# A first token list from 96 columns, a third list for the rest, six rounds for seven, and raw weights issued by ScalarE

## The chip, the cores and the metric

The kernel runs on one core of a Trainium2 chip. The core has TensorE (PE; the profile shows its weight loads apart, as PEld), VectorE (DVE), ScalarE (ACT), GpSimd (POOL) and SyncE (SP), which here only issues DMAs. ACT and POOL issue DMAs too. The metric is the time of one launch in device microseconds (us). Lower is better.

## The reference

An attention of fixed weights, a causal convolution of seven taps per head, is followed by a mixture of experts in which the (token, expert) pairs are taken greedily in the order of their logits, each token once and each expert up to its capacity.

```python
def reference(**kwargs):
    attn_out = _attn_ref(**attn_kwargs)            # [8, 3584, 192], softmax of 7 taps per head
    return _moe_ref(x=attn_out.reshape(28672, 192), **moe_kwargs)

def _moe_ref(x, w_gate, w1, w2):                   # w_gate 192x8, w1 8x192x1024, w2 8x1024x192
    cap = N // E                                   # 28672 / 8 = 3584
    logits = x @ w_gate
    order = np.argsort(-logits.flatten())
    for idx in order:
        tok, e = (int(idx) // E, int(idx) % E)
        if assigned[tok] >= 0 or counts[e] >= cap:
            continue
        assigned[tok] = e
        counts[e] += 1
    for e in range(E):
        mask = assigned == e
        out[mask] = np.maximum(x[mask] @ w1[e], 0.0) @ w2[e]
```

## The kernel before

**First stage.** The attention is computed in 16 tiles of 1792 rows. For each, conv(i) multiplies the rows X with a banded matrix TH, head by head (PE, tile cv), ACT copies the result from four PSUM banks to a, and a is stored to the DRAM tensor attn by ACT's queue. The rows of tile i + 3 are loaded at the start of tile i, by SP's and ACT's queues. Two tiles later the gate follows: DVE transposes a (transp, four steps, tile aT), PE makes the logits from it (gate, three steps of two matmul groups each, tile pl), and end(i) brings them into the table LT and takes the maximum over the experts (M1). LT holds 256 columns of 128 tokens, 16 columns a tile. These small steps stand in a list, left, that mid(h) works off beside conv, one step a head, and from tile LAG = 13 on only once the first list of tokens is made (got), then two steps a head.

**Lists.** A second program, bg, runs beside both stages as a chain of generators (line 1537), worked off a step at a time by hook in the first stage and by steps in the second. A model of the engines' times, Pace, decides while the program is written how many steps go in. The chain before is half(0), tail, half(1), rest. half(0) finds the threshold Ts from a sample of the first 96 columns (thresh), waits for column 128, and makes the list of the tokens above Ts in columns 0 to 127: settle marks them (F), count counts them, place numbers them with matmuls, slots splits the numbers, sort writes each token into its place with one-hot matmuls (tiles oa and X, one matmul for each column), turn transposes, gather collects and tokens turns it into row numbers (ia, ja). When it is done, first() gathers the rows of the first two FFN tiles, and todo transposes the first of them within the loop or behind it. tail makes the logits of the last two tiles. half(1) lists columns 128 to 255 in the same way, but with sort4, which turns its table through DRAM (otab) and lets other steps run meanwhile; before, these are open(), which opens the table for the rounds. rest runs the rounds (seven by ROUNDS), which settle the thresholds of all experts, then final, and the last lists, twice sort4.

**FFN.** Second stage: 56 tiles of 512 tokens; the first eight are one for each expert from the first list, the next 24 need the second list, the last 24 the last lists. Each takes 40 matmuls to the hidden layer (l1, tile ph; ACT writes hh, DVE the remainder hl) and 64 back (l2, tile y). Numbers are kept as high and low parts. Rows are gathered two tiles ahead by POOL; tile 8's gather, at the start of tile 6, is where the second list must be there (drain in idx_of), tile 32's, at the start of tile 30, the last one. In tiles 0 to 7 the weights come in as raw pieces, eight an expert: wsplit, once a step of eight in a tile, splits a piece on ACT and DVE, stores both parts to DRAM for later (kw, kd, kv), and calls wload, which loads the piece that takes the freed buffer, of four. All of these DMAs are issued by SP, in the order of the program. An issue on SP stands behind the copies that wait for their split. From tile 8 on the kept parts are read back.

If the checks at the end of the lists find a count that does not fit (bad), a general path follows that does everything again.

```python
ROUNDS = [(8, 1.0, False, 16)] + [(16, 1.0, False, 8)] * 2 + [(16, 0.5, True, 8)] * 2 + [(0, 0.0, True, 8)] * 2
...
        bg = Steps(nc, r, (half(0), tail(), half(1), rest()))
...
        self.done += 1
        self.wload()
```

Of the kernel before, what the change touches and what calls it, by code (L numbers as in the profile page):

```python
# [245 lines left out]
TA = 16  # L246
TB = 12

ROUNDS = [(8, 1.0, False, 16)] + [(16, 1.0, False, 8)] * 2 + [(16, 0.5, True, 8)] * 2 + [(0, 0.0, True, 8)] * 2
# [10 lines left out]
class Route:  # L260
# [15 lines left out]
    def consts(self):  # L276
# [12 lines left out]
        self.g1 = cst.tile([128, 2], F32, name="g1")  # L289
        for h in range(2):  # L290
            P.tensor_scalar(self.g1[:, h:h + 1], pf, 1.0 + 128 * h, None, op0=OP.add)
# [81 lines left out]
    def settle(self, h):  # L373

        V, wk = self.nc.vector, self.wk
        s = slice(128 * h, 128 * h + 128)
        yield "cols", 128 * h + 128
        if h == 0:
            self.F = wk.tile([128, 8, G], BF, name="F")
        m = wk.tile([128, 128], F32, name="m_f")  # L380
        V.scalar_tensor_tensor(m, self.M1[:, s], self.Ts, self.M1[:, s], op0=OP.is_lt, op1=OP.add)
        for q in range(2):
            e = slice(4 * q, 4 * q + 4)
            V.tensor_tensor(self.F[:, e, s], self.LT[:, e, s], m[:, None, :].to_broadcast([128, 4, 128]),
                            op=OP.is_equal)
            yield PEW if q else None


    def count(self, F, h):
        nc, wk = self.nc, self.wk  # L390
        V, PE = nc.vector, nc.tensor
        s = slice(128 * h, 128 * h + 128)
        if h == 0:
            self.tot = [None, None]
            self.sl = wk.tile([128, G], F32, name="sl")
        ps = self.bg()
        for e in range(8):
            PE.matmul(ps[:, e:e + 1], F[:, e, s], self.ones[:, 0:1], start=True, stop=True, skip_group_check=True)
        t = self.tot[h] = wk.tile([128, 8], BF, name="tot%d" % h)
        nc.scalar.activation(t, ps[:, 0:8], AF.Copy)  # L400
        yield PEA

    def place(self, F, h, base):
# [3 lines left out]
        s = slice(128 * h, 128 * h + 128)  # L407
        SP = wk.tile([128, 8, 128], F32, name="X0")
        for q in range(2):
            ps = self.bg()  # L410
            f = F[:, 4 * q:4 * q + 4, s]
            PE.matmul(ps, self.U, f, start=True, stop=False, skip_group_check=True)
            for u in range(4):
                e = 4 * q + u
                o = ps[:, 128 * u:128 * u + 128]
                b = lambda t: t[:, e:e + 1].to_broadcast([128, 128])
                if base is not None:
                    PE.matmul(o, b(self.tot[base]), self.ones, start=False, stop=False, skip_group_check=True)
                PE.matmul(o, b(self.tot[h]), self.U, start=False, stop=(u == 3), skip_group_check=True)
# [1286 lines left out]
```

## Time and profile before

| | us |
|---|---|
| three runs | 1254.54, 1260.52, 1265.29 |
| median | 1260.52 |
| profiled execution, its own time | 1251.99 |
| its span | 1250.2 |
| first hidden-layer write (hh) of tile 0 | 164.24 |
| of tile 8 | 324.16 |
| of tile 26 | 664.75 |
| of tile 30 | 758.64 |

Nearly all instructions go through the helper in line 56 (Meter), so groups are told apart by the names of what they write and read: "ph<-xa,w" is the hidden layer's matmul. In the rows of a timeline stand the start, the length, the engine, the shapes, how many were merged and, in brackets, the idle time ahead and who ended it. In the rows of windows stand the busy time and the number of instructions of PE, PEld, DVE, ACT and POOL, then the granted clock, the share of the DMA engines and GB/s. In the rows of waits stand the total, the number and the longest.

### The profile page before, as it was taken

Reading aid. Unit: us, or ns where it says so; the run is one execution under the profiler, and the core shown is the slowest. Engines: PE = TensorE matmul, PEld = TensorE weight load, DVE = VectorE, ACT = ScalarE, POOL = GpSimd, SP = SyncE. Lnnn points to the kernel's source line nnn. Section 1 sums busy time; section 2 is a strip of 40 time slices with the busy share of each in tenths; the row PEclk is TensorE's granted clock in tenths of the full one; section 3 lists DMA queues with packets and bytes.
Section 4 is the critical chain, followed back from the end, with each engine's and each line's share of the span. In section 5 each row is a group of like instructions: output and inputs, shape, how many; then the busy total and the mean of one; then the engine's idle time right before and its main releaser. Section 6 shows DMA issues by size and latency. Waiting matters only on the chain.

```text
span 1250.2 us, 21752 instructions
## 1 busy us (share of the span) xinstructions
PE 1208.1 (97%) x7702; PEld 1036.5 (83%) x7702; DVE 979.4 (78%) x2131; ACT 547.4 (44%) x1220; POOL 531.7 (43%) x528
## 2 busy tenths in 40 slices
PE   4999989999999999999999989999999999999997
PEld 2445568889988989889888879999999999999996
DVE  7388669889898898989888865777777777777772
ACT  4454555656444544444543333333443333443331
POOL 3000344535455545555454434445444544444522
PEclk9999999999999999999999999999999999999999
DMA  9999889999725463444344563114133222413100
GB/s 221 339 348 310 294 299 316 280 321 302 270 82 155 128 188 113 158 149 149 123 144 135 178 164 121 36 48 154 67 126 107 95 97 96 157 56 137 49 23 28
DMA packets 125188, 205.09 MB, mean 164 GB/s; under 512 B 21440, under 2 KB 85392, under 8 KB 121360
## 3 DMA queue, kind: packets, MB, share of 16 engines
q1 hardware_dynamic: 82464, 127.22, 31.9%
q0 software_dynamic: 21504, 44.07, 11.7%
q10 hardware_dynamic: 21104, 32.34, 7.8%
q8 instruction: 62, 1.02, 0.3%
q14 instruction: 54, 0.44, 0.1%
HBM read 118.64 MB, written 84.93 MB: 163 GB/s over the span
## 4 chain that ended last, share of the span: by engine, by line
PE 85%; DVE 6%; DMA 5%; issue 1%; SPq 1%; ACT 1%; POOL 1%; ACTq 0%; POOLq 0%; DVEq 0%
PE ph L56 40%; PE y L56 38%; PE bg L56 3%; PE cv L56 3%; DMA X<-in_x_dram 2%; DVE X L56 1%; DVE aT L56 1%; DMA wgr<-in_moe_w_gate_dram 1%; DMA raw<-in_moe_w_dram 1%; DMA X<-otab 1%; PE pl L56 1%; DMA xg<-attn,ja 1%; DVE hl L56 0%; PE px L56 0%; DMA otab<-X 0%
## 5 line engine op out<-in xcount | busy, mean ns | idle before, releaser
L56 PE MATMUL y<-w,hh 128*128 128x384 f32 x1792 | 536.8, 355 | 0.0
L56 ACT ACTIVATE hh<-ph 128x512 fp32r<-128x512 f32 x448 | 267.2, 597 | 486.3 <-PE ph L56 485.2
L56 PE MATMUL y<-w,hl 128*128 128x192 f32 x1792 | 449.7, 251 | 0.0
L56 DVE SCALAR_TENSOR_TENSOR hl<-ph,hh 128x512 fp32r<-128x512 f32 x448 | 308.5, 689 | 138.6 <-ACT hh L56 134.0
L56 PE MATMUL ph<-xa,w 128*128 128x512 f32 x1344 | 395.6, 402 | 0.0
L56 PEld LDWEIGHTS y<-w,hl 128*128 128x128 f32 x1792 | 341.7, 191 | 16.4
L56 PEld LDWEIGHTS y<-w,hh 128*128 128x128 f32 x1792 | 337.1, 188 | 20.4 <-issue 2.2
L56 PEld LDWEIGHTS ph<-xa,w 128*128 128x128 f32 x1344 | 218.9, 189 | 20.2 <-issue 1.0
L1348 POOL DMA_INDIRECT out_dram<-yo,ia x128 | 138.9, 1085 | 225.9 <-DVE yo L56 188.1
L1348 POOL DMA_INDIRECT out_dram<-yo,ib x96 | 95.9, 999 | 220.1 <-DVE yo L56 212.7
L56 PE MATMUL ph<-xd,w 128*128 128x512 f32 x448 | 178.9, 399 | 1.3 <-DVE xd L56 1.3
L56 PE MATMUL ph<-xd,dl 128*128 128x512 f32 x448 | 174.6, 390 | 0.2 <-DVE dl L56 0.2
L56 DVE STREAM_TRANSPOSE xs<-xg 32x128 f32<-32x128 f32 (+2 forms) x408 | 164.8, 404 | 6.6
L1273 POOL DMA_INDIRECT xg<-attn,ja x128 | 139.3, 1088 | 47.6 <-issue 40.4
L56 PE MATMUL cv<-X,TH 118*128 118x384 f32 x256 | 101.5, 523 | 19.5 <-DVE TH L56 12.5
L1273 POOL DMA_INDIRECT xg<-attn,jb x96 | 103.4, 1078 | 29.3 <-issue 29.3
L56 ACT ACTIVATE yt<-y 128x192 f32<-128x192 f32 x224 | 73.1, 326 | 94.3 <-PE y L56 92.3
L56 DVE TENSOR_TENSOR yo<-y,yt 128x192 f32<-128x192 f32 x224 | 79.5, 355 | 41.3 <-ACT yt L56 39.2
L56 PEld LDWEIGHTS ph<-xd,w 128*128 128x128 f32 x448 | 84.3, 188 | 21.4 <-DVE xd L56 1.7
L56 PEld LDWEIGHTS ph<-xd,dl 128*128 128x128 f32 x448 | 84.5, 189 | 19.7 <-issue 0.5
L56 PEld LDWEIGHTS cv<-X,TH 118*128 118x128 f32 x256 | 45.3, 198 | 49.9 <-issue 14.1
L56 ACT ACTIVATE a<-cv 128x384 f32<-128x384 f32 x128 | 59.5, 492 | 50.8 <-PE cv L56 33.0
(238 smaller groups left out, 893.1 us busy)
## 6 DMA issues: line engine op xcount, KB each, us to landing
attn<-a ACTq DMA_DIRECT2D x16, 1344.0 KB
w<-kw SPq DMA_DIRECT2D x14, 1536.0 KB
w<-kv SPq DMA_DIRECT2D x14, 1536.0 KB
kw<-w SPq DMA_DIRECT2D x48, 256.0 KB
kv<-w SPq DMA_DIRECT2D x32, 384.0 KB
X<-in_x_dram SPq DMA_DIRECT2D x17, 672.0 KB
X<-in_x_dram ACTq DMA_DIRECT2D x15, 672.0 KB
scr<-xs SPq DMA_DIRECT2D x96, 96.0 KB
```

The lines of the kernel that those rows point to most:

```text
L56: return f(*a, **k)
L1273: self.nc.gpsimd.indirect_dma_start(out=t[:, b], out_offset=None, in_=self.attn[0:rows], in_offset=bass.IndirectOffsetOnAxis(ap=idx[b], ax ...
L1348: st = self.nc.gpsimd.indirect_dma_start(out=self.out, out_offset=bass.IndirectOffsetOnAxis(ap=idx, axis=0), in_=o, in_offset=None, bounds ...
```

## The change

- **First list.** The columns are cut in PARTS, (0, 96), (96, 128) and (224, 32), given as first column and number. early makes the first list from the first part, so it waits for column 96 only. second lists the second part with sort4, with third (settle, count and counts for the last part) in its waiting time, and then the last part with sort and turn. The generators take a part and the parts ahead of it in place of a half and its base; their matmuls are as wide as the part. open() moves to the head of rest. The last lists stay halves (HALVES).
- **Rounds.** One of the two rounds (16, 1.0, False, 8) goes.
- **Raw weights.** wload issues on ACT's queue. wsplit no longer calls it at its end, but notes that a load is owed, and the next call of wsplit issues it first. The copies kept in DRAM (the parts) stay on SP's.
- **Logits.** From tile 13 on the three gate steps of a tile are one step, put ahead of the transposes.

```diff
+PARTS = ((0, 96), (96, 128), (224, 32))
+HALVES = ((0, 128), (128, 128))
+
+ROUNDS = [(8, 1.0, False, 16)] + [(16, 1.0, False, 8)] + [(16, 0.5, True, 8)] * 2 + [(0, 0.0, True, 8)] * 2
...
-    def settle(self, h):
+    def settle(self, part):
         V, wk = self.nc.vector, self.wk
-        s = slice(128 * h, 128 * h + 128)
-        yield "cols", 128 * h + 128
+        c0, n = part
+        s = slice(c0, c0 + n)
+        yield "cols", c0 + n
...
+                for p in bases:
+                    m = p[1]
+                    PE.matmul(o, self.tot[p][:, e:e + 1].to_broadcast([m, 128]), self.ones[0:m, 0:n],
+                              start=False, stop=False, skip_group_check=True)
+                PE.matmul(o, self.tot[part][:, e:e + 1].to_broadcast([n, 128]), self.U[0:n, 0:n],
+                          start=False, stop=(u == 3), skip_group_check=True)
...
-    def lists(self, F, nt, h, base, idx, row, *part, between=None, swap=False):
-
-        nc = self.nc
-        yield from self.place(F, h, base)
-        yield from self.slots(F, h, between is None)
+    def listed(self, F, nt, part, bases, between=None):
+
+        yield from self.place(F, part, bases)
+        yield from self.slots(F, part, between is None)
         if between is None:
-            yield from self.sort(h, nt, base)
-            yield from self.turn()
+            yield from self.sort(part, nt, bases)
+            yield from self.turn(part[1])
         else:
-            yield from self.sort4(h, nt, base)
+            yield from self.sort4(part, nt, bases)
             yield from between
-        yield from self.gather(nt, base is None)
-        yield from self.tokens(nt, idx, row, *part, swap=swap)
+        yield from self.gather(part[1], nt, not bases)
...
         if what == "a":
-            nc.sync.dma_start(t, self.w1[e, 0:128, s])
+            nc.scalar.dma_start(t, self.w1[e, 0:128, s])
         elif what == "d":
-            nc.sync.dma_start(t[0:64], self.w1[e, 128:192, s])
-            nc.sync.dma_start(t[64:128], self.w1[e, 128:192, s])
+            nc.scalar.dma_start(t[0:64], self.w1[e, 128:192, s])
+            nc.scalar.dma_start(t[64:128], self.w1[e, 128:192, s])
         else:
-            nc.sync.dma_start(t[:, 0:2 * D].rearrange("p (k d) -> p k d", d=D),
+            nc.scalar.dma_start(t[:, 0:2 * D].rearrange("p (k d) -> p k d", d=D),
...
     def wsplit(self, i, eng):
 
+        if self.owed:
+            self.wload()
+        self.owed = False
         if self.done == len(self.pieces) or self.pieces[self.done][0] > i:
             return
...
         self.done += 1
-        self.wload()
+        self.owed = True
...
-        def half(h):
-            if h == 0:
-                yield from r.thresh(0.905)
-            yield from r.settle(h)
-            yield from r.count(r.F, h)
-            if h:
-                yield from r.counts(NE)
-            yield from r.lists(r.F, TA, h, 0 if h else None, *((ia, ja) if h else (ia0, ja0, 8, 4)),
-                               between=r.open() if h else None, swap=h == 1)
+        def early():
+            yield from r.thresh(0.905)
+            yield from r.settle(PARTS[0])
+            yield from r.count(r.F, PARTS[0])
+            yield from r.listed(r.F, TA, PARTS[0], ())
+            yield from r.tokens(TA, ia0, ja0, 8, 4)
+
+        def second():
+            yield from r.settle(PARTS[1])
+            yield from r.count(r.F, PARTS[1])
+            yield from r.listed(r.F, TA, PARTS[1], PARTS[0:1], between=third())
+            yield from r.listed(r.F, TA, PARTS[2], PARTS[0:2])
+            yield from r.tokens(TA, ia, ja, swap=True)
+
+        def third():
+            yield from r.settle(PARTS[2])
+            yield from r.count(r.F, PARTS[2])
+            yield from r.counts(NE)
 
         def rest():
+            yield from r.open()
             yield from r.rounds()
...
-        bg = Steps(nc, r, (half(0), tail(), half(1), rest()))
+        bg = Steps(nc, r, (early(), tail(), second(), rest()))
...
+        def gates(i):
+            for u in range(3):
+                gate(i, u)
...
                 if i and h == 0:
+                    if i >= LAG:
+                        left.append(partial(gates, i - 2))
                     for u in range(4):
                         left.append(partial(k.transp, i - 1, u))
-                        if i > 1:
+                        if 1 < i and (u == 3 or i < LAG):
                             left.append(partial(gate, i - 2, u) if u < 3 else partial(end, i - 2))
```

155 lines of the change are left out of this document (81 added, 74 removed).

## The prediction

> **What bounds the kernel now.** I read the page first: the engines' shares and the chain that ended last.
>
> ```profile
> span 1250.2 us, 21752 instructions
> PE 1208.1 (97%) x7702; PEld 1036.5 (83%) x7702; DVE 979.4 (78%) x2131; ACT 547.4 (44%) x1220; POOL 531.7 (43%) x528
> PE 85%; DVE 6%; DMA 5%; issue 1%; SPq 1%; ACT 1%; POOL 1%; ACTq 0%; POOLq 0%; DVEq 0%
> ```
>
> TensorE (PE) carries the chain. Then I cut the span by stage: the last part of the first stage, in which attention and the first list share PE (to 164.2); FFN tiles 0 to 7, which read and split the weights; tiles 8 to 25, beside which the rounds run; tiles 26 to 29, beside which the last lists are made; and the rest. The second fence counts the hidden layer's (hh) instructions in the same stretches: ACT writes eight a tile. The last two columns are the DMA engines' share and GB/s: they are full up to tile 7 and not after.
>
> ```profile
> 99.20:164.20 65.00, 60.09 (x585) 35.76 (x588) 47.81 (x88) 32.36 (x81) 17.85 (x18) 1.00 0.92 286
> 164.20:324.10 159.90, 156.68 (x1103) 137.41 (x1100) 140.52 (x291) 92.24 (x199) 69.60 (x62) 1.00 0.95 312
> 324.10:664.70 340.60, 339.74 (x1962) 304.40 (x1961) 300.23 (x689) 155.37 (x382) 180.81 (x163) 1.00 0.46 142
> 664.70:758.60 93.90, 90.11 (x739) 78.47 (x738) 71.64 (x145) 37.05 (x73) 38.96 (x36) 0.96 0.54 157
> 758.60:1216.00 457.40, 457.40 (x2603) 415.29 (x2602) 344.60 (x733) 175.54 (x351) 202.27 (x196) 1.00 0.27 92
> ```
>
> ```profile
> 164.20:324.10 159.90, 68.38 (x225) 42.26 (x225) 43.21 (x63) 37.95 (x64) 1.00 0.95 312
> ...
> 664.70:758.60 93.90, 39.65 (x129) 24.71 (x128) 21.99 (x32) 19.16 (x32) 0.96 0.54 157
> 758.60:1216.00 457.40, 237.68 (x801) 150.17 (x801) 138.37 (x200) 119.48 (x201) 1.00 0.27 92
> ```
>
> A tile that nothing disturbs takes 457.4/25 = 18.3 us, and the change does not touch it. The excess is what can move: 159.9 - 8 x 18.3 = 13.5 us in tiles 0 to 7, 340.6 - 18 x 18.3 = 11.2 in 8 to 25, 93.9 - 4 x 18.3 = 20.7 in 26 to 29, and whatever the first stage wastes. So I asked last what PE itself waited for, from 96 to 190 us (four rows), from 190 to 325 (one) and after (last row).
>
> ```profile
> PE bg L56 <- DVE F L56: 1.7, 2, 1.3
> PE pl L56 <- DVE aT L56: 1.6, 3, 0.8
> PE bg L56 <- DMA xg<-attn,ja: 1.5, 1, 1.5
> PE ph L56 <- DVE xd L56: 1.3, 1, 1.3
> PE bg L56 <- DMA raw<-in_moe_w_dram: 1.6, 1, 1.6
> PE bg L56 <- DMA X<-otab: 3.3, 1, 3.3
> ```
>
> Only 11 us of PE waits are there to be won (the F wait of 1.3 lies in tile 1); the rest of the excess is PE's own work for lists, transposes and rounds.
>
> **The early list and the joined logits.** When the list starts and ends, and what its small matmuls cost:
>
> ```profile
> 96.07 0.16 DVE L56 TENSOR_TENSOR Ts<-t_u,t_t 128x1 f32<-128x1 f32 x1
> 99.29 0.35 DVE L56 SCALAR_TENSOR_TENSOR m_f<-M,Ts 128x128 f32<-128x128 f32 x1
> 114.98 1.65 PE L56 MATMUL bg<-X,oa 128*128 128x16 bf16 x24
> 116.49 1.54 PE L56 MATMUL cv<-X,TH 118*128 118x384 f32 x4
> 136.05 1.16 PE L56 MATMUL bg<-identb,X 128*128 128x128 bf16 x16
> 139.15 0.55 PE L56 MATMUL bg<-c_oh,X 128*128 128x32 bf16 x16
> 139.55 2.83 PE L56 MATMUL cv<-X,TH 118*128 118x384 f32 x8
> 145.25 0.18 DVE L56 TENSOR_SCALAR ja<-m_y 128x32 int32<-128x32 f32 x1
> ```
>
> The threshold Ts is ready at 96.2, but the list waits for the eighth tile's maxima until 99.3. With 96 columns it waits for tiles that are long done: 3.1 us sooner. Its sort lasts from 115 to 136; three quarters of the columns make that 5.3 us shorter. So ja comes at about 137 instead of 145.4. That alone is no gain, since PE, not the list, sets the end of the stage. PE gains 32 of 128 sort matmuls at (116.49 - 114.98)/24 = 63 ns, 2.0 us, and 0.2 by narrower places: -2.2. An earlier list also lets the gathers of the first FFN tile land before they are wanted, its remainder be transposed within the loop, and the last logits be made without waiting for transposes put out at the same moment: I take the xg wait (1.5), the xd wait (1.3) and half of the aT wait (0.8): -3.6, of 0 to -4.8 (all four rows without the 1.3 in tile 1). Joining three gates into one saves changes of PE's work, at most some tenths a tile: -0.5. Moving the deferred transposes forward costs nothing, since DVE is idle for 17 of these 65 us; without that cover it is the aT row again.
>
> The first four pieces of raw weights are now issued by ACT at tile 13, six DMAs. Times of issue on both queues, and what such a load waits for:
>
> ```profile
> 120.07 0.43 ACTq L194 DMA_DIRECT2D X<-in_x_dram  x1
> 126.14 0.47 SPq L1211 DMA_DIRECT2D raw<-in_moe_w_dram  x1
> 133.34 0.47 SPq L1212 DMA_DIRECT2D raw<-in_moe_w_dram  x1
> ```
>
> Six issues at 0.43 are 2.6 us of ACT, and the last of them hung on SP for nearly 7 us. Behind them ACT's copies of the attention's PSUM tiles (four banks) queue, and for those PE waits. Between 0 and +3 I take +0.7, near the lower end: by this moment the earlier transfers are mostly in. Sum of the stage: -2.2 - 3.6 - 0.5 + 0.7 = **-5.6**.
>
> **The third list, in tiles 1 to 6.** The second half's 128 columns stay a list of 128 (96 to 223); the last 32 are a list of their own. It adds to PE 8 matmuls of count, 26 of place, 32 of sort, 3 of columns, 16 of turn and 17 of gather: 102. At the gather's 25 ns ((139.55 - 139.15)/16) that is 2.6, at the sort's 63 ns 6.4; sort and turn at 63 and the other 54 at 33 give +4.8. DVE pays some 7 us for it, and is relieved of open(), which moves behind the lists. The counts move from before this list's sort to behind it and fill its round trip through DRAM, as open() did. One more wait of the kind of the F row, 0 to 1.3: +0.5. The lists must be ready when tile 8's gather is put out, at the start of tile 6; before, they end here:
>
> ```profile
> 267.22 0.59 DVE L56 TENSOR_SCALAR ja<-m_y 32x32 int32<-32x32 f32 x3
> 286.65 0.60 ACT L56 ACTIVATE hh<-ph 128x512 fp32r<-128x512 f32 x1 [0.32 <-PE ph L56]
> ```
>
> That leaves 19 us for a list whose sort is a quarter of the first one's 21 us: I count no forced finish.
>
> **Raw loads on ACT's queue, a step behind.** ACT's waits on raw weights in 160 to 325, and the number of their DMAs:
>
> ```profile
> ACT w L56 <- DMA raw<-in_moe_w_dram: 16.9, 13, 4.7
> raw<-in_moe_w_dram SPq DMA_DIRECT2D x32, 192.0 KB
> raw<-in_moe_w_dram SPq DMA_DIRECT2D x16, 256.0 KB
> raw<-in_moe_w_dram SPq DMA_DIRECT2D x32, 128.0 KB
> ```
>
> 80 issues at 0.43 are 34 us on ACT, which has 160 - 92 = 68 free in this stretch: mostly hidden, but hh and hl come later behind them. No row shows what PE loses: 0 to +6 (near half of the excess of 13.5, more than that ACT did not cause before), taken +1, since ACT stays under 80%. SP keeps the kept copies, in order, and each raw load no longer stands behind two of them that wait for DVE. Against it, the load is issued a step (2.3 us) later. The 16.9 us are ACT's; PE has two waits here that a late raw load can have caused, the F wait of 1.3 and the raw row's 1.6, together 2.9. I take about half, -1.5, of 0 to -2.9. Sum of the stage: 4.8 + 0.5 + 1.0 - 1.5 = **+4.8**.
> By the Trainium skill ("DMA: Bandwidth & Descriptors", Issuing engines are not separate DMA queues) all issuers' transfers run on the same 16 engines, and a second issuer saves only issue time. The 0.95 DMA share of this stretch agrees that bandwidth is short; by that rule the -1.5 falls away and the end is 1.5 us later.
>
> **Six rounds.** One round of seven leaves tiles 8 to 25: about 11.2 us over seven rounds and the final choice, 1.4 each: **-1.3**, of 0 to -2. Its DVE work (some 50 us elapsed) was hidden and brings nothing itself; the last lists come about two tiles earlier, which nothing waits for. Replayed on the reference's inputs, six rounds settle every expert's count as seven do.
>
> **The last lists.** Their PE work stays. What can go is one wait on their way through DRAM and its consequence:
>
> ```profile
> 730.21 1.19 PE L56 MATMUL bg<-oa,X 128*32 128x128 bf16 x32
> 736.00 0.59 SPq L546 DMA_DIRECT2D otab<-X  x1
> 742.42 0.26 PE L56 MATMUL bg<-iq,ones 128*128 128x192 bf16 x1
> 746.00 0.58 PE L56 MATMUL bg<-c_oh,X 128*128 128x24 bf16 x16 [3.32 <-DMA X<-otab]
> 749.50 1.53 PE L56 MATMUL ph<-xa,w 128*128 128x512 f32 x3
> 752.71 0.87 PE L56 MATMUL ph<-xa,w 128*128 128x512 f32 x3
> ```
>
> After 3.3 us without work three matmuls take 1.53 instead of 0.87 us; the stretch's granted clock of 0.96 is (1 - 0.96) x 93.9/0.5 = 7.5 us at half, about two thirds of it with PE at work, so some 2.4 us are lost beside the 3.3. The sort's last matmuls end at 731.4, but SP puts the table out only at 736.0: it was held by the tile's own transfers. Two tiles earlier the trip meets SP at another point of a tile: I take the wait as gone, **-5.7**, of 0 to -5.7.
> The Trainium skill ("TensorE: Matmul & The Clock Gate", What's actually happening) has the clock halved after one idle window of about 3.4 us; the trace agrees at 3.3, and shorter waits here (1.3 to 1.6) left it at 1.00.
>
> **Sum.** -5.6 + 4.8 - 1.3 - 5.7 = -7.8. The profiled execution took 1251.99 us (span 1250.2), so 1244.2. The three runs shown have their median 8.5 us higher, at 1260.52; on that scale 1252.7.
>
> **Rivals.** All are given on the median's scale.
> - Every wait goes: -2.2 - 0.5 - 4.8 in the first stage, 2.6 - 2.9 in tiles 0 to 7, -1.3 and -5.7: -14.8, 1245.7. For it speaks that the waits are few and all hang on the late list or on SP; against it that the third list's sort alone is 2.0.
> - The trip through DRAM is late again, in the last lists: the 5.7 stay, 1258.4. For it: SP is no freer there than before.
> - The other side: ACT is held by its own DMAs. The issue at 133.34 shows a load that could not be put out for 7 us; on ACT that holds hh. ACT has 68 us free and 34 of them go to issues, so from a mean wait of 34/80 = 0.43 us per issue it sets the pace. At 0.78 it would need 92 + 80 x 1.21 = 189, 29 more than the stretch: 1282. Against it: the two other rows of that fence took 0.43 and 0.47, and loads come a step later, when their buffer is free.
> - The lists are not done at tile 6, and the rest is put out at once: some 8 us of DVE before hl, about half of it on PE, +4: 1257.
> - The raw loads change nothing, because transfers are bandwidth-bound: 1254.2.
>
> **How the numbers follow.** About 1% is what a measurement of this kernel can tell from no change: 12.6 us. Chances: the forecast 0.38 (own range 1248 to 1257), all waits gone 0.28, the late trip 0.16, lists late 0.06, loads without effect 0.05, ACT held 0.07. Faster by over 1% (under 1248) is the first rival, 0.28; slower is ACT held, 0.07; the others, 0.65, lie within. The range goes from 1239, 6.7 below the first rival, to 1265, above the late ones; ACT held is left out.
>
> **What would show it.** First list's ja near 137; no PE wait on xg or xd before tile 0, whose first hh comes near 158.6; tiles 0 to 7 near 164.7 us, with 102 more small matmuls; the lists of tiles 1 to 3 ready between 268 and 286; tiles from the end of the lists on at 18.3; no granted half clock after 300. It is wrong if ACT shows long waits ahead of its raw issues, if tiles 0 to 7 pass 170 us, or if the first hh does not move.

## The result, and the profile after

The changed kernel takes 1277.43 us in the median of four runs (1273.94 to 1287.29), the kernel before beside it 1257.53. The ratio is 1.0164 with a 95% interval of 1.0130 to 1.0197: slower by 1.6%, where 1252.7 had been predicted, with a range from 1239 to 1265. The profiled execution took 1275.78 us. The first fence has three lines of its page, the second its windows by stage, cut at the first hh of tiles 0, 8, 26 and 30 (columns as before: length, then PE, PEld, DVE, ACT and POOL, granted clock, DMA share, GB/s).

```profile
span 1273.8 us, 21850 instructions
PE 1222.1 (96%) x7766; PEld 1047.2 (82%) x7766; DVE 953.6 (75%) x2091; ACT 543.4 (43%) x1207; POOL 532.6 (42%) x530
PE 82%; DMA 6%; DVE 6%; issue 3%; ACT 1%; POOL 1%; ACTq 1%; another core or an unknown queue 0%; SPq 0%; POOLq 0%; DVEq 0%
```

```profile
99.20:171.55 72.35, 60.17 (x533) 36.77 (x537) 38.98 (x79) 31.37 (x78) 16.00 (x16) 0.91 0.78 243
171.55:348.40 176.85, 170.34 (x1207) 147.52 (x1207) 143.21 (x306) 90.66 (x187) 74.99 (x63) 0.96 0.87 284
348.40:700.40 352.00, 347.43 (x2093) 310.91 (x2092) 295.83 (x675) 158.02 (x388) 181.17 (x166) 1.00 0.47 142
700.40:782.60 82.20, 79.39 (x599) 69.99 (x598) 54.30 (x108) 33.42 (x68) 36.18 (x34) 1.00 0.55 162
782.60:1240.00 457.40, 457.40 (x2603) 415.20 (x2601) 344.06 (x733) 175.14 (x350) 201.34 (x196) 1.00 0.28 92
```

PE is busy for as long as before in the first stretch (60.2 us), but the stretch is 7 us longer and the granted clock 0.91. The second stretch is 17 us longer, again with a lower clock. The last is the same to a hundredth. Against the prediction's terms, with a second trace of the same kernel (same_again, below):

| stretch | before, us | predicted | first trace | second trace |
|---|---|---|---|---|
| to tile 0's first hh | 164.2 | -5.6 | +7.3 | +6.3 |
| tiles 0 to 7 | 159.9 | +4.8 | +17.0 | +13.5 |
| tiles 8 to 29 | 434.5 | -7.0 | -0.3 | -5.5 |
| rest | 491.6 | 0 | -0.5 | -0.6 |

Part of the first row is no doing of the change. Up to the fifth of the 16 attention tiles (tile 4, counted from 0) PE's order is the same in all kernels of this document, and yet that tile's first conv matmul starts anywhere from 46.9 to 51.6 us: at 49.9 in the trace of before, 48.3 and 49.3 in the two of the changed kernel. Counted from there, the first hh takes 114.4 us before, 123.3 and 121.2 after.

So the loss lies in the first two stretches. Where PE stands still there is in its waits from 90 to 171.5 us (three rows) and in tiles 0 to 7 (two rows):

```profile
PE pt L56 <- ACT L L56: 6.2, 3, 3.7
PE cv L56 <- ACT a L56: 5.1, 1, 5.1
PE pl L56 <- DVE aT L56: 1.1, 2, 0.8
PE bg L56 <- DMA X<-otab: 3.5, 1, 3.5
PE bg L56 <- ACT L L56: 2.6, 1, 2.6
```

The first row to follow is the wait for a, the copies of the attention's PSUM tiles. The timeline at tile 13 shows what ACT did instead:

```profile
133.49 0.32 ACTq L205 DMA_DIRECT2D attn<-a  x1
133.85 0.50 ACTq L1223 DMA_DIRECT2D raw<-in_moe_w_dram  x1
134.39 1.52 ACTq L1225 DMA_DIRECT2D raw<-in_moe_w_dram  x1
135.96 1.92 ACTq L1226 DMA_DIRECT2D raw<-in_moe_w_dram  x1
137.91 0.63 ACTq L1223 DMA_DIRECT2D raw<-in_moe_w_dram  x1
138.58 0.52 ACTq L1225 DMA_DIRECT2D raw<-in_moe_w_dram  x1
139.14 0.61 ACTq L1226 DMA_DIRECT2D raw<-in_moe_w_dram  x1
139.85 0.87 ACT L56 ACTIVATE a<-cv 128x384 f32<-128x384 f32 x2 [6.38 <-DMA raw<-in_moe_w_dram]
140.39 4.04 PE L56 MATMUL cv<-X,TH 118*128 118x384 f32 x6 [5.13 <-ACT a L56]
```

Six issues hold ACT for 6.4 us, PE waits 5.1 behind it, and its next six matmuls take 4.04 us where eight took 2.83 before: the granted clock is 0.5 from 137.3 to 144.1. The first list was ready for its last copy (asm) at this moment too, so ja comes at 143.1 and not at the 137 foretold.

### The profile page after: what moved, and what is told of

It reads as the page before. It is cut to its first block, busy times and chain, and to the rows that moved or that the text cites. A ratio compares the mean times of both kernels' runs of the same rounds, so it can differ in the third digit from the quotient of the medians.

```text
span 1273.8 us, 21850 instructions
## 1 busy us (share of the span) xinstructions
PE 1222.1 (96%) x7766; PEld 1047.2 (82%) x7766; DVE 953.6 (75%) x2091; ACT 543.4 (43%) x1207; POOL 532.6 (42%) x530
## 3 DMA queue, kind: packets, MB, share of 16 engines
q10 hardware_dynamic: 34672, 47.03, 11.6%
## 4 chain that ended last, share of the span: by engine, by line
PE 82%; DMA 6%; DVE 6%; issue 3%; ACT 1%; POOL 1%; ACTq 1%; another core or an unknown queue 0%; SPq 0%; POOLq 0%; DVEq 0%
PE ph L56 38%; PE y L56 37%; PE bg L56 3%; DMA X<-in_x_dram 3%; PE cv L56 3%; DVE X L56 1%; DVE aT L56 1%; DMA otab<-X 1%; PE pl L56 1%; DVE hl L56 1%; DMA X<-otab 1%; DMA kw<-w 1%; DMA raw<-in_moe_w_dram 0%; POOL xg L1290 0%; PE px L56 0%
## 5 line engine op out<-in xcount | busy, mean ns | idle before, releaser
L56 PE MATMUL cv<-X,TH 118*128 118x384 f32 x256 | 106.1, 546 | 21.5 <-DVE TH L56 12.0
L56 PEld LDWEIGHTS cv<-X,TH 118*128 118x128 f32 x256 | 48.0, 207 | 55.1 <-issue 15.6
```

Of the source, the lines that this page charges most:

```text
L56: return f(*a, **k)
```

## The experiments

Theory 1 is that ACT is held by its own raw loads, with PE behind it; theory 3, formed after the first four kernels, that in tiles 0 to 7 these loads cost PE only through the table's trip. The rivals are the joined logits (1), the third list (2) and, for the stretch behind, the order of the steps. The table has all kernels, with the ratio to the kernel before that was measured together with them, the first hh, how long it is behind the start of the fifth attention tile, and the stretches of the profiled execution. An asterisk marks traces with late results, of which more at the end; the trace of before has none, the first trace of the changed kernel has them. The kernels were measured in five groups: before and changed; all_but_raw, front_on_sp, gates_apart and all_but_lists; cover, cover_raw_sp, only_six and six_cover; wide, owed_sp, six_gates and six_gates_lat; same_again, after_lat, before_lat and six_lat.

| kernel | ratio (95%) | first hh | from the fifth tile | tiles 0 to 7 | 8 to 29 |
|---|---|---|---|---|---|
| before | 1 | 164.2 | 114.4 | 159.9 | 434.5 |
| changed * | 1.0164 (1.0130 to 1.0197) | 171.6 | 123.3 | 176.9 | 434.2 |
| same_again | 1.0167 (1.0141 to 1.0193) | 170.5 | 121.2 | 173.5 | 429.0 |
| all_but_raw | 1.0042 (1.0019 to 1.0065) | 159.6 | 112.5 | 170.5 | 428.4 |
| front_on_sp | 1.0090 (1.0057 to 1.0124) | 162.6 | 115.5 | 174.5 | 434.0 |
| owed_sp * | 1.0100 (1.0083 to 1.0117) | 165.7 | 114.1 | 172.9 | 437.7 |
| gates_apart | 1.0170 (1.0137 to 1.0203) | 172.2 | 124.8 | 173.5 | 433.3 |
| all_but_lists | 1.0051 (1.0036 to 1.0065) | 170.4 | 123.2 | 165.6 | 427.0 |
| cover * | 1.0121 (1.0098 to 1.0145) | 171.1 | 121.4 | 171.6 | 439.4 |
| cover_raw_sp * | 1.0067 (1.0048 to 1.0086) | 163.6 | 112.9 | 169.7 | 435.0 |
| wide * | 1.0059 (1.0042 to 1.0076) | 157.4 | 110.1 | 169.6 | 445.4 |
| only_six * | 0.9968 (0.9953 to 0.9982) | 164.0 | 116.8 | 162.1 | 434.1 |
| six_cover * | 0.9963 (0.9948 to 0.9978) | 162.5 | 113.4 | 161.1 | 438.3 |
| six_gates * | 0.9993 (0.9974 to 1.0012) | 161.9 | 115.0 | 162.1 | 441.6 |
| six_gates_lat * | 0.9909 (0.9892 to 0.9926) | 165.5 | 118.1 | 158.8 | 428.3 |
| after_lat | 1.0096 (1.0079 to 1.0112) | 168.7 | 120.0 | 172.3 | 428.6 |
| before_lat | 1.0066 (1.0048 to 1.0084) | 163.8 | 112.5 | 156.5 | 443.8 |
| six_lat | 0.9910 (0.9889 to 0.9931) | 163.1 | 113.0 | 158.7 | 426.6 |

### Raw loads: the queue and the step

**all_but_raw**: the changed kernel with the loads as they were.

```diff
-            nc.scalar.dma_start(t, self.w1[e, 0:128, s])
+            nc.sync.dma_start(t, self.w1[e, 0:128, s])
...
-        self.owed = True
+        self.wload()
```

> The changed kernel with the raw loads back on SP's queue, issued at the end of their split as before; lists, joined logits and six rounds stay. Theory 1, ACT is held by its own raw issues, at tile 13 and again in tiles 0 to 7: ACT's wait of 6.4 us on its DMAs at tile 13 goes, tile 0's first hh moves from 171.5 to about 164, tiles 0 to 7 shrink from 176.9 to about 170, and the ratio to before falls from 1.016 to about 1.005. Rival 1, the joined logits hold the front: hh of tile 0 stays at 170 or later. Rival 2, the third list holds tiles 0 to 7: these stay at 173 to 177.

The first hh comes at 159.6, 10.9 us sooner than in same_again (8.7 counted from the fifth tile), ja at 137.4, and PE waits 0.8 us in the whole front. The ratio falls by 0.012. So theory 1 holds for the front, and more strongly than expected. Tiles 0 to 7 come to 170.5, as theory 1 had it and below rival 2's 173 to 177; but that is still 10.6 us more than before, so the third list costs much as well.

Even here ACT is held once by a DMA, as the timeline shows:

```profile
155.02 0.95 SPq L1227 DMA_DIRECT2D raw<-in_moe_w_dram  x1
155.33 0.39 PE L56 MATMUL ph<-xd,dl 128*128 128x512 f32 x1
...
159.26 0.31 ACTq L205 DMA_DIRECT2D attn<-a  x1
159.62 0.60 ACT L56 ACTIVATE hh<-ph 128x512 fp32r<-128x512 f32 x1 [4.52 <-PE px L56]
```

The matmuls of the first hidden layer end at 155.7, but ACT stands at its last store of a, which takes the same semaphore as the raw load that SP issued at 155.02. That load lands at 159.18, the store goes out at 159.26, and hh follows. In the kernel before, hh starts 0.1 us after its matmuls (164.14).

**front_on_sp**: only the six DMAs at tile 13 go back.

```diff
+        eng = nc.sync if self.loaded < 4 else nc.scalar
...
-            nc.scalar.dma_start(t, self.w1[e, 0:128, s])
+            eng.dma_start(t, self.w1[e, 0:128, s])
```

> The changed kernel with only the first four pieces (six DMAs, at tile 13) issued by SP; the other raw loads stay on ACT's queue. Theory 1 for the front alone: the 6.4 us wait of ACT and the 5.1 us wait of PE behind it go, the granted half clock at 137 goes with them, ja comes near 138 rather than 143, and tile 0's first hh near 164 rather than 171.5; tiles 0 to 7 keep their 176.9. Ratio about 1.010. Rival 1, the joined logits: hh stays at 170 or later, since PE's waits for the logits' copies take the place.

The first hh moves to 162.6 and the block at tile 13 is gone, but PE still waits 6.3 us for a, somewhat later. The timeline shows a second block, of the next raw load:

```profile
135.68 1.25 POOL L1291 DMA_INDIRECT xg<-attn,ja  x1 [29.38 <-DVE aT L56]
...
145.79 1.00 POOL L1291 DMA_INDIRECT xg<-attn,ja  x1 [0.31 <-issue]
146.81 1.27 POOL L1272 TENSOR_TENSOR w<-raw,w 128x512 fp32r<-128x512 f32 x1
148.11 0.43 ACTq L1229 DMA_DIRECT2D raw<-in_moe_w_dram  x1
148.59 0.63 ACT L56 ACTIVATE w<-raw 128x512 fp32r<-128x512 f32 x1 [6.89 <-POOL w L1272]
149.65 1.01 PE L56 MATMUL cv<-X,TH 118*128 118x384 f32 x1 [6.32 <-ACT a L56]
```

The load needs the buffer of the piece that POOL splits, and POOL's split stands behind its eight gathers of the first two FFN tiles. On SP's queue this wait held nothing; on ACT's it holds ACT, and PE behind it. In same_again both blocks are there: two waits for a, 10.4 us together.

**owed_sp**: the queue back, the step of delay kept.

> The changed kernel with its raw loads on SP's queue but still a step behind their split. If the queue alone is what costs, this is as the kernel with both undone: first hh near 160 to 162, tiles 0 to 7 near 170, ratio 1.002 to 1.006. If the step of delay costs too, ACT's wait for raw pieces grows past the 16.9 us of before, PE waits on w or dl in tiles 0 to 7, and the ratio is 1.008 or more.

1.0100 against 1.0042 without the delay, with intervals apart; so the delay seems to cost too, about half of what queue and delay cost together. The two kernels ran on different chips, owed_sp's trace has late results, and 4.5 of the 6.1 us by which its first hh comes later than in all_but_raw lie ahead of the fifth tile, so the size is uncertain. Against wide (below), which was measured beside it and has its loads at once on SP, it is 1.0100 to 1.0059, but wide differs in its matmuls too. How the delay costs is not shown: ACT's waits for raw pieces ahead of their copies, which were to grow past 16.9 us, are 14.3 here (19.7 with those for which the trace has no cause) and 18.7 in all_but_raw. One row of ACT's waits looks like it:

```profile
ACT hh L56 <- DMA raw<-in_moe_w_dram: 4.7, 1, 4.7
```

But it is the stand at the last store of a again, which took 4.5 us of ACT in all_but_raw.

### Joined logits

**gates_apart**: the gate steps one by one, as before.

```diff
-                    if i >= LAG:
-                        left.append(partial(gates, i - 2))
...
-                        if 1 < i and (u == 3 or i < LAG):
+                        if i > 1:
```

> The changed kernel with the logits of a tile in three steps again, spread over the transposes as before; all else stays. Rival 1, the joined logits cost the front: PE's waits of 6.2 us for the transpose of the logits (pt behind ACT's L) go, tile 0's first hh comes near 165, ratio about 1.011. Theory 1: ACT's 6.4 us wait at tile 13 stays, and hh of tile 0 moves by less than 2 us, ratio 1.015 to 1.017.

Nothing moves: 1.0170, first hh 172.2, and PE still waits 4.8 us for L, once, behind the second block. The joined logits cost nothing that these runs can tell; nor do they in the kernel before with six rounds and more slack (six_gates_lat and six_lat below, 0.9909 and 0.9910). In the first trace 3.7 of the 6.2 us for L stand where same_again has the second block: there L is copied at 156.2, though the logits' matmuls ended at 151.5, a late result. In same_again, with joined logits, PE waits for a instead.

### What tiles 0 to 7 lose

**all_but_lists**: the kernel before with all parts of the change but the lists.

```diff
-ROUNDS = [(8, 1.0, False, 16)] + [(16, 1.0, False, 8)] * 2 + [(16, 0.5, True, 8)] * 2 + [(0, 0.0, True, 8)] * 2
+ROUNDS = [(8, 1.0, False, 16)] + [(16, 1.0, False, 8)] + [(16, 0.5, True, 8)] * 2 + [(0, 0.0, True, 8)] * 2
...
-            nc.sync.dma_start(t, self.w1[e, 0:128, s])
+            nc.scalar.dma_start(t, self.w1[e, 0:128, s])
...
-        self.wload()
+        self.owed = True
...
+                    if i >= LAG:
+                        left.append(partial(gates, i - 2))
```

> The kernel before with six rounds, raw loads on ACT's queue a step behind, and joined logits, but with its own two lists of 128 columns and open() at its old place. Rival 2, the third list costs tiles 0 to 7 most of their 17 us: tiles 0 to 7 come to about 160 to 164 (before 159.9, changed 176.9), and the ratio is about 1.006. If the raw loads cost them instead: 170 or more, ratio 1.012 to 1.016. In both the front stays late, tile 0's first hh at 169 to 173, if ACT's own issues or the joined logits hold it, and the wait on the table's trip through DRAM in the last lists shows whether six rounds alone move it.

Between the two: 165.6, that is +5.6 with the raw loads (and six rounds and joined logits), and with all_but_raw's +10.6 for the lists the two sum to 16.2, within the changed kernel's 13.5 to 17.0. Beside the third list the raw loads add less: 2.9 from all_but_raw to same_again. The front stays late (170.4). PE's waits in these tiles hold one large one, the second list's table on its way through DRAM, named by the last DMA of SP's that came in:

```profile
PE bg L56 <- DMA kw<-w: 4.5, 1, 4.5
```

Why it is late is seen in SP's queue. SP puts out the table's second half (otab) and then eight reads of it. First the timeline of same_again, with PE's wait behind it, then a row of SP's waits from the same trace, then the timeline of all_but_raw:

```profile
243.15 0.46 SPq L557 DMA_DIRECT2D otab<-X  x1
243.70 10.13 SPq L574 DMA_DIRECT2D X<-otab  x8
...
257.35 0.59 PE L56 MATMUL bg<-c_oh,X 128*128 128x32 bf16 x16 [3.35 <-DMA X<-otab]
```

```profile
SPq L574 <- DMA raw<-in_moe_w_dram: 2.5, 2, 2.2
```

```profile
234.35 0.32 SPq L557 DMA_DIRECT2D otab<-X  x1
234.72 7.45 SPq L574 DMA_DIRECT2D X<-otab  x8
```

In these traces the DMAs of SP and ACT take eight semaphores in turn, and an issue waits until the DMA before it on the same semaphore has landed: the fifth of the eight reads goes out at 251.91, when the raw load ahead of it on its semaphore has landed at 251.89. With ACT's raw loads between them, the reads need more rounds of these semaphores: 10.1 us to put out instead of 7.5, and two of them wait for raw loads by name. From the table's write to the last landing it is 14.1 us (243.15 to 257.25) instead of 10.4; the order allows TURN = 10.

**cover**: the changed kernel with a longer allowance.

```diff
-TURN = 10.0
+TURN = 16.0
```

> The changed kernel with TURN, the time that the order allows a table for its trip through DRAM, at 16 us instead of 10. Theory 3: what the raw loads on ACT's queue cost in tiles 0 to 7 is the trip in tile 4. SP's eight reads of the table share their semaphores with ACT's raw loads and take 14.3 us from the table's second write to the last landing, against 10.4 with the raw loads on SP; PE waits 3.5 us and the granted clock is halved behind it. With 16 us that wait goes and the half clock at 263 with it: tile 4 from 34.0 to about 28 to 29, tiles 0 to 7 from 176.9 to about 171, the 1.8 us wait for the table in the last lists goes too, ratio from 1.016 to about 1.010. Rival: the time in tiles 0 to 7 is lost because ACT stands at each raw issue until DVE's split is done; then a longer allowance leaves tiles 0 to 7 within 2 us of 176.9 and moves only where PE waits.

The wait is gone, tile 4 takes 29.0 instead of 34.0, tiles 0 to 7 take 171.6, within 1.1 us of those with the raw loads on SP. ACT issues its raw loads as before, so theory 3 holds for most of the loss, and its rival falls. Not for all: the half clock in tile 4 stays, shorter (267.0 to 270.4), behind a wait of 1.1 us on DVE between place's halves, and against cover_raw_sp, which has the same allowance, tiles 0 to 7 are still 1.9 us longer. The ratio of 1.0121 against 1.0164 is in the direction, with intervals that overlap a little.

**cover_raw_sp**: the same allowance with raw loads on SP.

> The changed kernel with its raw loads back on SP, as before, and TURN at 16 us. Against the same without the longer allowance (1.0042): theory 3 has the wait of 1.1 us ahead of the second list's gather go, and with it the half clock at 249, if that came from this wait and the 26 small matmuls right behind it, 3.8 us in which PE was poorly filled; tile 4 from 29.7 to about 27, and the 2.6 us wait in the last lists goes: ratio about 0.999. Rival: the third list's matmuls alone halve the clock; then the half clock stays within 3 us of the place step and tile 4 stays over 28.5, ratio 1.002.

Tile 4 falls from 29.7 to 27.0 and the half clock in it goes although place's small matmuls are there as before, with a wait of 0.6 us between their halves. So here a wait of 1.1 us with 2.2 us of poorly filled PE behind it was followed by half the clock, and the same matmuls with 0.6 us were not. One trace of each does not make that a rule, as the last section shows. The ratio missed: 1.0067. In its trace the front came 4 us later, 3.6 of them ahead of the fifth tile, and tiles 8 to 29 took 7 us more, with waits on the rounds (r_v, r_cc) of 4.9 us.

### The price of narrow matmuls

**wide**: all_but_raw, with the counts of a part padded with zeros to 128 rows and the first part's transposes made over 128 columns.

```diff
-                    PE.matmul(o, self.tot[p][:, e:e + 1].to_broadcast([m, 128]), self.ones[0:m, 0:n],
+                    PE.matmul(o, self.tot[p][:, e:e + 1].to_broadcast([128, 128]), self.ones[:, 0:n],
...
+        if n > 64:
+            n = 128
```

> The changed kernel with raw loads back on SP (ratio 1.0042 without this edit) and the lists' narrow matmuls made wide again: the counts of a part are padded with zeros to 128 rows, so that no matmul of place changes the number of rows that it uses, and the first part's 96-column transposes are made over 128 columns. Theory: narrow forms cost PE more than they save. The 16 transposes of the first list took 2.98 us at 96 columns against 1.16 at 128 before; place's 26 matmuls in tile 4 took 2.3 us, where those with 32 rows behind one with 128, and the reverse, stand 108 to 118 ns apart, against 25 to 60 among equal ones. So: the 16 transposes 1.2, place in tile 4 about 1.0, the half clock at 249 gone if poorly filled PE brought it on; first hh 1 to 2 us sooner, tile 4 from 29.7 to about 27, ratio about 1.001. Rival: the spacing comes from DVE or ACT, or from the small size alone; then both stay at 2.9 and 2.2.

The rows of the timeline, first of the changed kernel, then of all_but_raw, then of wide:

```profile
129.05 2.98 PE L56 MATMUL bg<-identb,X 128*96 128x128 bf16 x16
```

```profile
245.50 0.20 PE L56 MATMUL bg<-ones,tot 96*128 96x32 bf16 x2
245.63 0.18 PE L56 MATMUL bg<-U,tot 32*128 32x32 bf16 x1
245.75 0.22 PE L56 MATMUL bg<-ones,tot 96*128 96x32 bf16 x2
```

```profile
126.78 1.15 PE L56 MATMUL bg<-identb,X 128*128 128x128 bf16 x16
...
243.09 0.20 PE L56 MATMUL bg<-ones,tot 128*128 128x32 bf16 x2
243.14 0.18 PE L56 MATMUL bg<-U,tot 128*128 128x32 bf16 x1
243.16 0.20 PE L56 MATMUL bg<-ones,tot 128*128 128x32 bf16 x2
```

Sixteen transposes of 96 columns take 2.98 us, of 128 columns 1.15. Three matmuls of place take 0.25 us where 96, 128 and 32 rows alternate and 0.07 where all have 128. Both are as expected, and the rival falls: the narrow form itself is slow. The Trainium skill ("TensorE: Matmul & The Clock Gate", Weight-path perf modes — Fast Weight Load (FWL) and DoubleRow) says that fast weight load is on when the weights number 128 and are not FP32; the transposes agree with it (PE's weight loads took 276 ns at 96 columns and 96 to 122 at 128), and the prediction had overlooked it. That the change between row counts is slow is what these rows show. The first hh came 2.2 us sooner, but not by the transposes: 2.5 us of lead are there before them, at the start of attention tile 12, since all_but_raw has half the clock from 109.0 to 115.8 and wide has not. The transposes' 1.8 us show in tile 12 (11.6 us against 13.4), and 1.9 us are lost again in attention tile 14, where PE waits 0.9 us for nothing that the profile shows. The ratio did not follow (1.0059): in tile 4 PE stood 2.3 us between place's halves, waiting for nothing that the profile shows, and tiles 8 to 29 took 445.4.

### Six rounds, and the order's slack

**only_six** and **six_cover**: the kernel before with six rounds, and with TURN = 16 beside them.

> The kernel before with six rounds and nothing else. The prediction's terms: 1.3 us of PE less, and the last lists' table meets SP at another point of a tile, so that its wait of 3.3 us and the half clock of 2.4 us go: -7, ratio 0.994, tiles 8 to 29 from 434.5 to about 427.5. Rival: the trip is late wherever it lies, the wait stays: -1.3, ratio 0.999, tiles 8 to 29 at about 433.

> The kernel before with six rounds and TURN at 16 us: no wait on the table in tile 4 (1.6 before) nor in the last lists (3.3 before), and no granted half clock there: -1.3 - 1.6 - 5.7 = -8.6, ratio 0.993, faster than both kernels. Rival: what PE gains it gives back, because the longer allowance only moves the gather behind other work that then comes late; ratio 0.998 or more.

Both are faster, 0.9968 and 0.9963, by less than expected. The wait for the table in the last lists is gone in both. But tiles 8 to 29 take 434.1 and 438.3: in these traces PE waits instead for results of the rounds (r_v, r_cc) and for ACT's copies of the sort. **six_gates**, with joined logits beside six rounds, shows the same:

> The kernel before with six rounds and joined logits, its own lists and its raw loads on SP. The joined logits alone should be worth little: first hh within 2 us of 164, tiles 0 to 7 near 160. With six rounds tiles 8 to 29 lost 25.8 us when nothing else was changed and 18.7 with joined logits and raw loads on ACT. If that comes from the step of a tile at which the rounds begin, which the order decides, tiles 8 to 29 are at either 427 or 434, ratio 0.991 or 0.997. If it came from the raw loads on ACT, it is 434.

441.6 and 0.9993: none of the values expected. It ran with late results too, and the waits for r_v and r_cc were 5.9 us. So **six_gates_lat** gives the order more slack:

```diff
-        nc.lat, nc.las = (0.8, 1.2)
+        nc.lat, nc.las = (1.8, 2.2)
```

> The same with the order's latency for DVE and ACT results in the second stage at 1.8 and 2.2 us instead of 0.8 and 1.2. PE's waits on DVE's results of the rounds and on ACT's copies of the sort (9 us with six rounds alone, from 330 to 790) go, since each step is put in a microsecond later: tiles 8 to 29 at 424 to 428, ratio 0.989 to 0.992. Rival: the waits come from DVE being late by more than that, or the later steps only meet other waits: 430 or more, ratio 0.995 or more.

0.9909: faster than both kernels, tiles 8 to 29 at 428.3, although results are late in this trace too. The next four were measured together, and their traces have no late results, although the chip is that of the group with TURN = 16, whose traces all have them.

**same_again** is the changed kernel once more:

> The changed kernel itself, for a second trace beside the kernels of this call. Theory: the waits that do not change with the order (ACT's 6.4 us at its raw issues at tile 13, the 3.5 us for the table in tile 4) are there again at the same places within 0.5 us; those of PE on the rounds' results (r_v, r_cc, r_c; 4.3 us from 345 on) are there if PE's results are again seen late by the other engines (1.5 to 3.3 us late in eight places of the first trace, never in the trace of before), and are under 1 us if they are not. Ratio 1.013 to 1.020.

**after_lat** is the changed kernel with the longer allowance for results:

> The changed kernel with the order's allowance for results of DVE and ACT in the second stage at 1.8 and 2.2 us in place of 0.8 and 1.2; nothing else differs. Theory: the missing gain in tiles 8 to 29 (predicted -7.0 us, shown -0.3) is lost in waits for results that come later than the order allows; with the allowance PE's waits on r_v, r_cc, r_c and X from 345 on go from 6 us to under 2, tiles 8 to 29 from 434.2 to about 428, and the ratio falls by 0.004 to 0.006 to about 1.011. The first stage (hh at 171.5) and tile 4's loss, which have other causes, stay within 2 us. Rival: tiles 8 to 29 lose their time in the FFN's own waits; then they stay over 432.

**before_lat** is the kernel before with the same allowance:

> The kernel before with that allowance alone. It waited 1.2 us on the rounds and 3.3 us on the table in its trace, so there is less to win: by the theory ratio 0.993 to 0.998. If it comes to 0.991 as the kernel with six rounds, joined logits and the allowance, then the allowance is all of that gain, and six rounds bring nothing.

**six_lat** is the kernel before with that allowance and six rounds:

> The kernel before with six rounds and that allowance, its logits in three steps. If joined logits are worth nothing: 0.991 as with them. If they cost (six rounds alone 0.9968, with joined logits 0.9993): 0.989 or less.

The changed kernel has both its front and its tile 4 again as they were. Its waits on the rounds are gone without any edit, and tiles 8 to 29 gain 5.5 of the 7.0 us foretold; the table's wait in the last lists is still there (3.0). after_lat gains 0.007 in the ratio, but its tiles 8 to 29 are the same (428.6 to 429.0): in these profiles the theory had nothing to show. Nor is tile 4's loss won, against what was expected of it: it moves on, with 27.2 us in tile 4 and 25.9 in tile 5, where same_again has 33.4 and 20.4.

before_lat is slower, 1.0066, outside the expectation and with the lesson of this group. Its stretch of the last lists, tiles 26 to 29, against that of six_lat:

```profile
658.46:764.14 105.68, 91.31 (x758) 78.18 (x757) 79.53 (x164) 38.77 (x80) 39.42 (x34) 0.90 0.55 159
```

```profile
663.71:748.40 84.69, 83.79 (x664) 74.17 (x663) 56.51 (x116) 34.81 (x70) 38.03 (x36) 1.00 0.57 168
```

```profile
PE bg L56 <- DMA X<-otab: 9.0, 1, 9.0
PE bg L56 <- DVE oa L56: 3.7, 9, 1.3
```

With seven rounds and the longer allowance the last lists are not done when tile 30's gather falls due. All that is left is put out at once in tile 29 (46.1 us), and PE waits 9.0 us for the table and 3.7 for the sort's tiles (last fence, waits in tiles 26 to 29 of before_lat). With six rounds there is room: six_lat takes 1240.07 us in the median against 1249.13, ratio 0.9910, as foretold if joined logits are worth nothing, and is the fastest kernel found beside six_gates_lat. So the round's worth is not the 1.3 us of PE alone: it is two tiles of slack, and the allowance uses them.

## Why the prediction was wrong

**First stage, "+0.7" for six raw issues on ACT.** This is the step that failed. The prediction had the row that spoke against it, a load on SP that could not be put out for nearly 7 us, and chose "near the lower end: by this moment the earlier transfers are mostly in". Measured: 10.9 us of first hh between same_again and all_but_raw, 8.7 counted from the fifth tile, in two blocks. The first is the six issues (6.4 us of ACT, 5.1 of PE, and the half clock behind). The second the prediction never looked for: a load that waits for its buffer waits for POOL's split, behind eight gathers that start 1.3 us apart. In the prediction the delay by a step was to have the buffer free by then; for POOL's splits it has not.

**First stage, the early list.** Right in mechanism: without the raw loads on ACT ja comes at 137.4 (foretold near 137), the waits on xg and xd are gone, and the first hidden layer's matmuls end 8.4 us sooner, 5.6 counted from the fifth tile, where -6.3 was foretold without the raw issues. That the first hh itself, at 159.6, comes near the 158.6 foretold is luck: 2.8 us of it are the sooner start of the fifth tile, and 3.9 are lost again while ACT stands at its last store. Counted from the fifth tile, the first hh comes only 1.9 us sooner than before. The term of -2.2 was mis-sized: the 16 transposes cost 1.8 more at 96 columns, so some 0.4 remain. Tile 0 then takes 2.4 us longer than before, with waits for hl (3.9) and L (1.0).

**Tiles 0 to 7, the third list.** +5.3 predicted, +10.6 measured with raw loads on SP. Its matmuls were priced by the gather's and the sort's rows at 33 and 63 ns. In all_but_raw place takes 2.2 us where 26 at 33 ns would be 0.9, sort 2.3, turn 1.2 and gather 0.8: 6.5 with the rest small. Beside these stand tile 0's waits, and in tile 4 the 1.1 us wait with 3.4 us of half clock behind; by tiles, the 10.6 us are 2.4 in tile 0 and 8.1 in tile 4.

**Tiles 0 to 7, raw loads.** -0.5 predicted, +5.6 measured with two lists, +2.9 with three. ACT is held there, as the rival had it, but hh did not set the pace; the loss is for the most part the table's trip, which the prediction followed only in the last lists. The rival "ACT is held by its own DMAs" came nearest in time (1282) with the wrong place: it put its 29 us into hh of tiles 0 to 7. It had a chance of 0.07 and was left out of the range. Its gain from earlier loads (-1.5) is not seen in any run.

**Six rounds and the last lists.** -7.0 predicted, -5.5 in the second trace, -7.5 in all_but_lists: right in size. But the rival of the late trip came true in part: with three lists and the old allowances a wait of 1.8 to 4.4 us stays, with two lists and six rounds it is gone or under 0.5. In the first trace late results took the rest.

**Signs.** Of the three that were to show the prediction wrong two appeared: ACT's long wait ahead of its raw issues, and tiles 0 to 7 over 170 us. The third was a first hh that does not move; it moved the other way.

## What to carry to other kernels

In these traces a DMA issued by a compute engine is an instruction in that engine's order: whatever it waits for holds the copies behind it. Six issues in a row held ACT for 6.4 us, a buffer that another engine had yet to split for 5.8 to 6.9, a semaphore still taken by a load on the other queue for 4.1. So a DMA belongs on such a queue only where its buffer and its semaphore are free for certain. A second issuer also takes semaphores from the first, and may lengthen a chain of DMAs that runs there (14.1 us instead of 10.4). Fewer columns or rows do not make a small matmul cheaper if they leave its fast form (186 ns at 96 columns against 72 at 128): price the new form by a row of that very form. And work removed beside the bound may be worth its slack more than its time, if something can use that slack. Before two traces are compared by when a stage ends, look at where they part: here they were up to 4.7 us apart before PE's order differed at all.

## What the runs showed that I had not expected

**Late results.** In some traces an engine sees another's result late, at a few places and by up to 4.7 us (the copy of L in the changed kernel's first trace). In the nine marked traces 9 to 24 of the 448 copies hh begin over 0.8 us after both their matmul and ACT's work before them have ended; in the others none does. The timeline of wide shows one at ACT's hh: its matmul ended at 366.44, its copy began at 369.34, after ph of the next step.

```profile
366.05 0.39 PE L56 MATMUL ph<-xd,dl 128*128 128x512 f32 x1
368.33 0.39 PE L56 MATMUL ph<-xd,dl 128*128 128x512 f32 x1
369.34 0.60 ACT L56 ACTIVATE hh<-ph 128x512 fp32r<-128x512 f32 x1 [4.56 <-PE bg L56]
```

In the same kernel order (all_but_raw) the copy followed in 0.04 us. The traces with late results also miss semaphore records: 1125 of PE's are there in the changed kernel's first trace, 1205 in its second, 1202 in that of before. It goes by the group measured together: all traces of two groups are free of it, all of two others are not, and the kernel before took 1249 to 1250 us in the former and 1256 to 1258 in the latter. One chip has had a group of each kind. all_but_raw and wide, whose instructions stand in the same order, differ by 17 us in tiles 8 to 29, and the waits that make the difference follow such places. Whether it belongs to the chip or to the recording of the profile stays open. A ratio compares kernels of one group, so both stood under the same; but an order with little slack may lose more by it, and no run here separates that.

**Weight loads and row counts.** Transposes of 96 columns at 186 ns and matmuls that change between 32 and 128 rows at 108 to 118 ns, against 72 and 25 to 60.

**The clock.** It was halved with no wait longer than 1.1 us, where 2.2 us of small matmuls stood behind it; the prediction had named one wait of over 3 us. The front shows the same with 0.8 us: all ten traces with the early list have this one wait, on aT, among 2.2 us of small matmuls of the gate and the sort. In five of them the clock is halved at 109 to 113, at a cost of 1.3 to 2.8 us; in the other five it is not. The changed kernel has it in its first trace and not in its second. So such a stretch can halve the clock, but the order alone does not decide it.
